# Two cached decode attentions on one core: the keys of the second loaded whole in 64 KB rows, with part of them copied aside by GpSimd, and its softmax taken in two halves

## The chip, the core and the metric

The kernel runs on one core of one Trainium2 chip. A core has a matrix engine (TensorE, PE in the profile), a vector engine (VectorE, DVE), a scalar engine (ScalarE, ACT), GpSimd (POOL) and SyncE (SP), which issues transfers. They share the on-chip memories SBUF (128 partitions) and PSUM (where PE writes), and 16 DMA engines bring data from HBM into SBUF. Engines run their own instruction lists and wait for each other by semaphores. The metric is the device time of one execution in microseconds (us).

## The reference

Two independent attention steps for one new token, A and B, each for a batch of 4, 32 query heads and a head size of 128, in bf16. Their results are laid side by side in the output of shape (4, 1, 1024).

```
q = (x @ wq) split into 32 heads
scores = q . k / sqrt(128);  p = softmax(scores);  o = p . v;  result = concat(o) @ wo
A: 8 key/value heads (each shared by 4 query heads), the last 2048 of 8192 cached positions
B: 32 key/value heads, all 8192 cached positions
```

B's caches are 256 MB of keys and 256 MB of values (4 x 32 x 8192 x 128 in bf16 each), so nearly all of the kernel is the reading and use of B's caches.

## The kernel before, in words

The work is cut into 40 chunks. Chunks 0 to 7 are A's. Chunks 8 to 39 are B's (the code's `NCA` is 8 and `NC` is 40): each is four heads of one batch entry, so 256 key tiles and 256 value tiles of 128 x 128. Four chunks in a row (the four batch entries) share one slice of B's output weights, `wos`, of 0.5 MB.

SBUF holds one long buffer `kv` of ten slots, 16 KB in each partition. In part B the keys of a chunk fill slots 0 to 3 (64 KB in each partition), the values slots 4 to 7; slot 8 holds `wol`, the reordered output weights. There is one buffer for keys and one for values. The keys come as two transfers of half a chunk, so in rows of 32 KB, the values as one transfer in rows of 64 KB. Only the last chunks are loaded in more pieces (`LASTK`, `NEXTK`, `LASTV`, `NEXTV`), so that their use can begin earlier.

SP issues all these transfers in the order of the chunks, keys before values, and each waits until the part of the buffer that it overwrites has been used: a half of the keys until the transposes of that half of the chunk before are done, the values until the last product with the values of the chunk before is done. POOL does nothing in part B but pass landings on: it waits for a transfer's semaphore and raises a counter (`r_k`, `r_v`; `relay`, L70) that PE waits for.

`whole_B` (L796) writes one chunk for all engines:

- For each group of 8 key tiles (32 groups), PE transposes the tiles into one of three PSUM banks `tr` (`emit_T`, L465), DVE (two groups of three) or ACT (the third) copies the bank to `kt` in SBUF (L486, L484), and two groups later PE multiplies them with the query into the scores `sc` (`emit_S`, L503). DVE also copies the query of the chunk into `qq` (`emit_qb`, L491).
- After the last scores the softmax follows over the whole chunk. `stats_rowmax` (L546) takes the maxima per partition of both halves, `stats_gmax` (L561) turns them by PE and reduces them, `stats_bc` (L579) spreads the maximum of each head to its partitions, and `exp_B` (L595) takes the exponentials, 8 instructions on ACT. While that runs, PE reorders the output weights (`reorder`, L706, 16 matmuls in all; DVE copies the result to `wol`, `take_wol`, L714) and does 11 matmuls on constants that only keep it busy (`keep_busy`, L791).
- PE multiplies the probabilities with the 256 value tiles (`emit_pv`, L643), DVE sums the probabilities (`sums_B`, L605), PE sums over partitions (`norm_sum`, L662) and DVE scales the result (`norm_out`, L680).
- The product with the output weights (`emit_fin`, L719) is done by PE two groups into the next chunk, and for the last chunk behind the loop.

The order is written out by hand. `emit_looped` (L156) looks for equal stretches between the marks set by `mark` and makes a loop of each engine's equal chunks; on PE and DVE one loop covers all 32 chunks of B. What differs between chunks only by steps of semaphore values is put into registers.

The lines that the steps of the prediction touch are L363 to L411 (transfers of B and their order), L465 to L489, L546 to L607, L643 to L717 and L796 to L832.

Of the kernel before, what the change touches and what calls it, by code (L numbers as in the profile page):

```python
# [5 lines left out]

ACTF = mybir.ActivationFunctionType
# [5 lines left out]
P = 128  # L13
# [9 lines left out]
LASTK = (32, 32, 64, 64, 64)  # L23
NEXTK = (64, 64, 64, 64)
NEXTV = (128, 64, 32, 32)
LASTV = (128, 64, 32, 16, 8, 8)
QK = (0, 4, 8, 16, 24)
QV = (0, 16, 24, 28, 30, 31)

# [139 lines left out]
def bass_concat_heads__sliding_block_cached__mha_block_cached__decode_kernel(  # L169
# [42 lines left out]
    assert sum(LASTV) == sum(LASTK) == sum(NEXTK) == sum(NEXTV) == NTB and NTA * 16 == 1024 and NTB * 4 == 1024  # L212

    sch = _Sched()
    with ExitStack() as es:
# [26 lines left out]
        rh = sb("rh", [P, 2, 4], F32)  # L242
# [4 lines left out]
        rst = {0: sb("rsa", [P, NSM, 16], F32), 1: sb("rsb", [P, 4], F32)}  # L247
# [3 lines left out]
        pbt = {0: sb("pba", [P, NPB, NTA * 16 + NW], BF16), 1: sb("pbb", [P, 1, NTB * 4 + NW], BF16)}  # L251
# [6 lines left out]
        wol = kv[:, 8, 0:4 * DO].rearrange("p (u n) -> p u n", u=4)  # L258
        tr = ps("tr", [P, NTRB, TG * P], BF16)
# [4 lines left out]
        xtps = ms[:, XT0:XT0 + KC * NB].bitcast(BF16)  # L264

        semnames = ["eng_pe", "eng_dve", "eng_act", "eng_pool", "eng_sp", "d_x0", "d_x1", "d_o0", "d_o1", "r_k", "r_v"]
        semnames += ["d_h%d" % i for i in range(NH)] + ["d_bk0", "d_bk1", "d_bv0"]
        semnames += [f + str(i) for f, x in (("d_lk", LASTK), ("d_nk", NEXTK), ("d_lv", LASTV), ("d_nv", NEXTV)) for i in range(len(x))]
# [79 lines left out]
        def dma_wos(hq):  # L348


            src = B_wo[4 * hq * P:4 * (hq + 1) * P, :].rearrange("(p r) n -> p (r n)", r=4)
            sch.add_dma("sp", lambda e: e.dma_start(wos[:, :, :].rearrange("p r n -> p (r n)"), src), "d_wos",
                        waits=[("reord", NCA + 4 * hq - 1)] if hq else [], key=("wos", hq))
# [9 lines left out]
        def dma_B(kind, c, part=None):  # L363


            ch = chunks[c]
            T, at, steps = (B_k, KB, QK) if kind == "k" else (B_v, VB, QV)
            src = T[ch["b"], 4 * ch["hq"]:4 * ch["hq"] + 4].rearrange("u (pp j) d -> (u pp) (j d)", pp=P // 4)
            dst = flat(at, 4)
            if kind == "k":  # L370
                pieces, fam = (LASTK, "d_lk") if c == NC - 1 else (NEXTK, "d_nk") if c == NC - 2 else ((NTB // 2,) * 2, "d_bk")
            else:
                pieces, fam = (LASTV, "d_lv") if c == NC - 1 else (NEXTV, "d_nv") if c in (NC - 2, NC - 3) else ((NTB,), "d_bv")
            j0, unit, used = 0, NTB // 4, {}
            for i, n in enumerate(pieces):
                if part is not None and i != part:
                    j0 += n
                    continue
                waits = []
                for u in range(j0 // unit, (j0 + n - 1) // unit + 1):  # L380
                    waits += held[at + u]
                    used[at + u] = [("T", ch["s"] + (u + 1) * unit // TG - 1) if kind == "k" else ("pv", c)]
                x = slice(j0 * P, (j0 + n) * P)
                sch.add_dma("sp", lambda e, x=x: e.dma_start(dst[:, x], src[:, x]), fam + str(i), waits=waits, key=(kind, c, i))
                j0 += n
                sch.relay("pool", sems, "r_" + kind, n // TG, [(kind, c, i)] + ([("wos", ch["hq"])] if i == 1 and kind == "k" and ch["b"] == 0 else []))
            for g, end in zip(steps, steps[1:] + (NTB // TG,)):
                sch.tk[(kind + "r", c, g)] = ("r_" + kind, (c - NCA) * (NTB // TG) + end)
            for u in used:
                held[u] = used[u]  # L390
# [527 lines left out]
```

## Time and profile before

| | |
|---|---|
| device time, 3 runs | median 1375.0 us (1374.14 to 1376.61) |
| profiled execution, first to last instruction (its span) | 1371.8 us |
| PE busy, share of the span | 1249.8 us, 91% |
| DVE busy | 744.0 us, 54% |
| ACT busy | 513.8 us, 37% |
| POOL busy | 9.8 us, 1% |
| read from HBM | 587.21 MB, 428 GB/s over the span |

The profile gives one execution and its span; the 3.2 us between the span and the median of the runs lie around it. In the rows that follow, times are in us from the start of the span. A row of the timeline gives the start, the length, the engine, the line, the operation, what is written from what, how many instructions were merged, and in brackets how long the engine had been idle before and what released it. "issue" as a releaser means that nothing that the profile shows was waited for. PE is the matrix product, PEld its loading of weights. A row of a window gives, for each engine, its busy time and instructions, then the granted clock of PE (1.00 is full), the mean busy share of the DMA engines and their rate.

### The profile page before, as it was taken

Reading aid. Unit: us, or ns where it says so; the run is one execution under the profiler, and the core shown is the slowest. Engines: PE = TensorE matmul, PEld = TensorE weight load, DVE = VectorE, ACT = ScalarE, POOL = GpSimd, SP = SyncE. Lnnn points to the kernel's source line nnn. Section 1 sums busy time; section 2 is a strip of 40 time slices with the busy share of each in tenths; the row PEclk is TensorE's granted clock in tenths of the full one; section 3 lists DMA queues with packets and bytes.
Section 4 is the critical chain, followed back from the end, with each engine's and each line's share of the span. In section 5 each row is a group of like instructions: output and inputs, shape, how many; then the busy total and the mean of one; then the engine's idle time right before and its main releaser. Section 6 shows DMA issues by size and latency. Waiting matters only on the chain.

```text
span 1371.8 us, 61526 instructions
## 1 busy us (share of the span) xinstructions
PE 1249.8 (91%) x27769; PEld 1110.4 (81%) x27769; DVE 744.0 (54%) x1335; ACT 513.8 (37%) x649; POOL 9.8 (1%) x29
## 2 busy tenths in 40 slices
PE   4897999998999999999999999999999999998998
PEld 4786788888778787888777888888778889877887
DVE  1675456655545556555555555554555555554555
ACT  1553244433333344333333443333333433333333
POOL 2000000000000000000000000000000000000000
PEclk9998899999999999999999999999999999999999
DMA  9999999999999999999999999999999999999998
GB/s 398 427 426 444 417 422 431 432 437 441 428 438 428 423 434 434 431 438 440 428 428 424 438 431 429 445 432 428 434 429 429 430 438 438 434 430 429 422 428 340
DMA packets 21084, 587.52 MB, mean 428 GB/s; under 512 B 2356, under 2 KB 2376, under 8 KB 4808
## 3 DMA queue, kind: packets, MB, share of 16 engines
q1 hardware_dynamic: 21032, 587.21, 99.6%
q8 instruction: 15, 0.25, 0.1%
q14 instruction: 5, 0.04, 0.0%
q10 hardware_dynamic: 32, 0.01, 0.0%
HBM read 587.21 MB, written 0.01 MB: 428 GB/s over the span
## 4 chain that ended last, share of the span: by engine, by line
DMA 57%; PE 39%; DVE 2%; issue 1%; ACT 0%; SPq 0%; POOLq 0%; DVEq 0%
DMA kv<-in_B_k_cache_dram 36%; DMA kv<-in_B_v_cache_dram 18%; PE tr L419 18%; PE po L421 9%; PE sc L421 8%; DMA kv<-in_B_wq_dram 2%; PE fin L421 1%; PE ms L421 1%; PE tr L421 1%; DMA kv<-in_A_k_cache_dram 1%; DVE sA L539 1%; DVE kt L486 0%; DVE kv L716 0%; ACT pba L623 0%; DVE rm L551 0%
## 5 line engine op out<-in xcount | busy, mean ns | idle before, releaser
L419 PE MATMUL tr<-identb,kv 128*128 128x128 bf16 x8704 | 668.6, 221 | 48.2 <-POOLq L72 42.3
L486 DVE COPY kt<-tr 128x1024 bf16<-128x1024 bf16 x736 | 501.9, 691 | 264.0 <-PE tr L419 261.3
L484 ACT ACTIVATE kt<-tr 128x1024 bf16<-128x1024 bf16 x352 | 359.3, 1023 | 703.5 <-PE tr L419 703.4
L419 PEld LDWEIGHTS tr<-identb,kv 128*128 128x128 bf16 x8704 | 510.3, 99 | 61.1 <-DVE qq L495 41.2
L421 PE MATMUL sc<-qq,kt 128*128 128x64 bf16 x8192 | 399.3, 192 | 13.5 <-DVE kt L486 9.8
L421 PEld LDWEIGHTS sc<-qq,kt 128*128 128x128 bf16 x8192 | 332.9, 98 | 16.9 <-DVE kt L486 13.1
L421 PEld LDWEIGHTS po<-pbb,kv 128*128 128x128 bf16 x8192 | 250.9, 99 | 37.1 <-issue 20.5
L421 PE MATMUL po<-pbb,kv 128*128 128x64 bf16 x8192 | 253.8, 194 | 24.1 <-POOLq L72 22.6
L601 ACT ACTIVATE pbb<-sc,negb 32x128 bf16<-32x128 f32 x256 | 137.8, 538 | 136.3 <-DVE negb L584 133.0
L421 PE MATMUL po<-sel,identb 128*128 128x512 bf16 x352 | 96.9, 384 | 0.0
L716 DVE CAST kv<-tr 128x512 bf16<-128x512 f32 x128 | 80.0, 683 | 0.0
L606 DVE TENSOR_REDUCE rsb<-pbb 128x4 f32<-128x1024 bf16 x32 | 39.0, 1220 | 65.8 <-ACT pbb L601 65.8
L421 PE MATMUL tr<-wos,back 32*128 32x512 bf16 x512 | 67.8, 383 | 3.2
L421 PEld LDWEIGHTS po<-sel,identb 128*128 128x128 bf16 x352 | 26.6, 98 | 47.6 <-issue 27.8
L668 DVE RECIPROCAL rinv<-ms 128x4 f32<-128x4 f32 (+1 forms) x40 | 7.8, 196 | 105.6 <-PE ms L421 105.6
L555 DVE TENSOR_REDUCE rh<-sc 128x4 f32<-128x512 f32 x64 | 43.9, 686 | 14.3 <-PE sc L421 14.3
L421 PEld LDWEIGHTS tr<-wos,back 32*128 32x128 bf16 x512 | 21.5, 93 | 34.0 <-DVE kv L716 18.9
L690 DVE TENSOR_TENSOR oz<-po,rz 128x16 bf16<-128x16 f32 x32 | 5.6, 175 | 67.9 <-PE po L421 67.9
L570 DVE TENSOR_REDUCE gm<-ms 4x4 f32<-4x128 f32 x40 | 11.2, 279 | 28.6 <-PE ms L419 28.6
L421 PE MATMUL sc<-qb,kt 128*128 128x64 bf16 (+3 forms) x512 | 26.3, 197 | 0.4 <-DVE gx L576 0.4
L421 PEld LDWEIGHTS ms<-gm,ind 4*128 4x128 f32 x64 | 9.4, 182 | 17.5 <-DVE gm L570 17.5
L421 PEld LDWEIGHTS sc<-qb,kt 128*128 128x128 bf16 x512 | 22.1, 102 | 1.6 <-issue 0.9
(65 smaller groups left out, 250.4 us busy)
## 6 DMA issues: line engine op xcount, KB each, us to landing
kv<-in_B_k_cache_dram SPq DMA_DIRECT2D x60, 4096.0 KB, 27.4
kv<-in_A_k_cache_dram SPq DMA_DIRECT2D x8, 2048.0 KB, 13.0
kv<-in_A_v_cache_dram SPq DMA_DIRECT2D x8, 2048.0 KB, 14.6
kv<-in_B_k_cache_dram SPq DMA_DIRECT2D x7, 2048.0 KB, 28.4
kv<-in_B_v_cache_dram SPq DMA_DIRECT2D x3, 4096.0 KB, 22.3
kv<-in_B_v_cache_dram SPq DMA_DIRECT2D x3, 2048.0 KB, 26.8
kv<-in_B_v_cache_dram SPq DMA_DIRECT2D x5, 1024.0 KB, 29.6
kv<-in_A_wq_dram SPq DMA_DIRECT2D x1, 4096.0 KB, 12.5
```

Of the source, the lines that this page charges most:

```text
L419: sch.add("pe", lambda e: e.transpose(o, l, r), waits, key)
L421: sch.add("pe", lambda e: e.matmul(o, l, r, start=start, stop=stop), waits, key)
L484: sch.add("act", lambda e: e.activation(dst, src, ACTF.Copy), waits=waits, key=("ev", s))
L486: sch.add("dve", lambda e: e.tensor_copy(dst, src), waits=waits, key=("ev", s))
L539: emit = lambda e, src=src, b=b: e.scalar_tensor_tensor(out=t, in0=src, scalar=mk[:, b:b + 1], in1=t, op0=ALU.mult, op1=ALU.add)
L555: sch.add("dve", lambda e: e.tensor_reduce(out=rh[:, half, :], in_=src, axis=AX.X, op=ALU.max), waits=[("S", ch["s"] + (half + 1) * ch["NG ...
L570: sch.add("dve", lambda e: e.tensor_reduce(out=gm[0:C, m, 0:U], in_=src, axis=AX.X, op=ALU.max), waits=[("trm", c)], key=("gmax", c))
L601: sch.add("act", lambda e, src=src, dst=dst, pp=pp, u=u: e.activation(dst, src, ACTF.Exp, bias=negb[pp, 0, u:u + 1], scale=scale), waits=[ ...
L606: sch.add("dve", lambda e: e.tensor_reduce(out=rst[1][:, :], in_=probs_of(c).rearrange("p j u -> p u j"), axis=AX.X, op=ALU.add), waits=[( ...
L668: sch.add("dve", lambda e: e.reciprocal(out=ri, in_=ms[:, L0:L0 + n]), waits=[("L", c)], key=("rinv", c))
L690: sch.add("dve", lambda e: e.tensor_tensor(out=o, in0=i0, in1=i1, op=ALU.mult), waits=waits, key=("oT", c))
L716: sch.add("dve", lambda e: e.tensor_copy(wol[:, u, :], o), waits=[("reord", c) if u == 3 else ("reord", c, u)] + [("fin", prev(c))], key=( ...
```

## The change

- B's keys are loaded as one transfer of 8 MB in rows of 64 KB for 26 of the 32 chunks (9 to 34). Chunk 8 comes in pieces of 128, 32 and 96 tiles, chunks 35 to 38 in pieces of 64, 96 and 96, chunk 39 in 32, 32, 96 and 96. Values come in pieces of 128, 64 and 64 tiles in chunks 35 to 38.
- A second place `kspare` for the last 96 key tiles of a chunk lies in slots 8 and 9. After a whole load has landed, POOL copies these 96 tiles there in 12 instructions of 8 tiles (`land_kB`), and PE transposes them from there. So the load of the next keys waits for the transposes of the first 160 tiles and for the 12 copies of the chunk before; in chunks with pieces, the last 96 tiles are loaded into `kspare` directly.
- The softmax of a chunk has two halves. The first half's maximum is taken while the transposes go on, and its exponentials (groups 23 and 26) too. The second half uses the larger of both maxima. The products with the values of the first half (in `po`) start right behind the last scores; those of the second half go to another bank (`po2`, in `tr`). A factor from the difference of the two maxima (`weigh_B`) brings the first half's sums and products to the scale of the second (`rest_sums`, `norm_sum`, `add_first`).
- The output product of a chunk (`emit_fin`) is now at the end of the same chunk, followed by all 16 matmuls of `reorder` for the next chunk and 3 `keep_busy` matmuls; `take_wol` stands at the head of the next chunk on DVE. The first three transposes of a chunk wait for `take_wol`.
- The query copy of a chunk moves from DVE to ACT. POOL's relays are listed in a loop of their own, with one more counter for `wos`. In the changed program PE's loop covers 31 of B's chunks; the last chunk is written out behind it, since the product that closes the sum in `emit_fin` (`stop`) now lies inside it.

The core of the diff:

```diff
-LASTK = (32, 32, 64, 64, 64)
-NEXTK = (64, 64, 64, 64)
-NEXTV = (128, 64, 32, 32)
+KMAIN = 160
+FIRSTK = (128, 32, 96)
+LATEK = (64, 96, 96)
+LASTK = (32, 32, 96, 96)
+NLATE = 5
+NEXTV = (128, 64, 64)
...
+        kspare = kv[:, 8:10, :].rearrange("p s x -> p (s x)")[:, 4 * DO:4 * DO + (NTB - KMAIN) * P]
...
+        po2 = tr[:, 2, :].bitcast(F32)
...
+        def kpieces(c):
+            return FIRSTK if c == NCA else LASTK if c == NC - 1 else LATEK if c >= NC - NLATE else (NTB,)
...
+                    dst = flat(KB, 4)[:, j0 * P:(j0 + n) * P]
+                    if c == NCA:
+                        waits = held[0] + held[1] + held[2] + held[3]
+                    else:
+                        waits = [("T", s0 + min(j0 + n, KMAIN) // TG - 1)]
+                        if j0 + n > KMAIN and len(kpieces(c - 1)) == 1:
+                            waits += [("cp", c - 1)]
...
+        def land_kB(c):
...
+                if len(pieces) == 1:
+                    sch.relay("pool", sems, "r_k", KMAIN // TG, [("k", c, i)])
+                    for g in range(NCP):
+                        x = slice((KMAIN + g * TG) * P, (KMAIN + (g + 1) * TG) * P)
+                        dst, org = kspare[:, g * TG * P:(g + 1) * TG * P].bitcast(I32), flat(KB, 4)[:, x].bitcast(I32)
+                        sch.add("pool", lambda e, dst=dst, org=org: e.tensor_copy(dst, org), waits=[("T", s0 + ch["NG"] - 1)] if g == 0 else [])
+                        emit, waits, _, at = sch.ops["pool"][-1]
+                        sch.ops["pool"][-1] = (emit, waits, ("r_c", 1), at)
...
+        def weigh_B(c):
+
+            sch.add("dve", lambda e: e.tensor_tensor(out=e01[:, :], in0=negb[:, 1, :], in1=negb[:, 0, :], op=ALU.subtract),
+                    waits=[("negb", c, 1)] + ([("rse", c - 1)] if c > NCA else []), key=("d01", c))
+            sch.add("act", lambda e: e.activation(e01[:, :], e01[:, :], ACTF.Exp), waits=[("d01", c)], key=("e01", c))
...
+        def add_first(c):
+
+            pe_mm(po2[:, 0:4], identf[:, :], t1[:, :], start=False, stop=False, waits=[("t1", c)], key=("add", c))
+            po_read[:] = [("t1", c)]
...
         def whole_B(c):
...
             sch.mark()
+            take_wol(c)
             emit_qb(c)
             for g in range(ch["NG"]):
                 emit_T(ch["s"] + g)
-                if g == 1:
-                    emit_fin(p)
                 if g >= SLAG:
                     emit_S(ch["s"] + g - SLAG)
-                if g == ch["NG"] // 2 + SLAG + 1:
+                if g == 18:
                     stats_rowmax(c, 0)
+                if g == 20:
+                    stats_gmax(c, 0)
+                if g == 22:
+                    stats_bc(c, 0)
+                if g == 23:
+                    exp_B(c, 0, (0, 1))
+                if g == 26:
+                    exp_B(c, 0, (2, 3))
             for g in range(SLAG):
                 emit_S(ch["s_last"] + 1 - SLAG + g)
             stats_rowmax(c, 1)
-            reorder(c, 0, 0)
-            reorder(c, 1, 1)
-            reorder(c, 2, 2)
-            keep_busy(2)
-            stats_gmax(c)
-            keep_busy(1)
-            stats_bc(c)
-            exp_B(c)
-            for u in range(3):
-                take_wol(c, u, u)
-            keep_busy(3)
-            reorder(c, 3, 0)
-            keep_busy(5)
-            take_wol(c, 3, 0)
-            sums_B(c)
             for g in range(ch["NG"]):
                 emit_pv(c, g)
-                if g == 20:
+                if g == 4:
+                    stats_gmax(c, 1)
+                if g == 8:
+                    stats_bc(c, 1)
+                    sums_B(c, 0)
+                    exp_B(c, 1, (0, 1, 2, 3))
+                    weigh_B(c)
+                    sums_B(c, 1)
+                    rest_sums(c)
+                if g == 24:
                     norm_sum(c)
+                if g == ch["NG"] - 2:
+                    add_first(c)
             norm_out(c)
+            emit_fin(c)
+            reorder(c + 1)
+            keep_busy(NBUSY)
...
         finish_A()
+        reorder(NCA)
         for c in range(NCA, NC):
             whole_B(c)
         sch.mark()
-        emit_fin(NC - 1)
+        emit_out(NC - 1)
```

284 lines of the change are left out of this document (176 added, 108 removed).

## The prediction

> **What bounds the kernel now.** I read the page first: the slices of the DMA engines and the share of the queue that loads the caches.
>
> ```profile
> span 1371.8 us, 61526 instructions
> ...
> DMA  9999999999999999999999999999999999999998
> ...
> q1 hardware_dynamic: 21032, 587.21, 99.6%
> ```
>
> Every slice but the last has the DMA engines busy at 90% or more, and the loading queue fills 99.6% of 16 engines over a span of 1371.8 us. Nothing that only makes an engine faster can shorten this. The time is the bytes, the price of their packets, gaps in the queue, and what follows the last byte. To see how late PE may be, I read PE's timeline over one chunk of B in mid run.
>
> ```profile
> 672.88 1.06 PE L419 MATMUL tr<-identb,kv 128*128 128x128 bf16 x16 [1.85 <-POOLq L72]
> ...
> 695.76 1.06 PE L421 MATMUL tr<-wos,back 32*128 32x512 bf16 x12
> ...
> 699.08 1.03 PE L421 MATMUL tr<-wos,back 32*128 32x512 bf16 x4
> ...
> 701.96 5.06 PE L421 MATMUL po<-pbb,kv 128*128 128x64 bf16 x168 [0.67 <-POOLq L72]
> ...
> 711.66 0.51 PE L419 MATMUL tr<-identb,kv 128*128 128x128 bf16 x6 [1.85 <-POOLq L72]
> ```
>
> The chunk lasts from 672.88 to 711.66, 38.78 us. PE waits only for landings that POOL passes on: 1.85 us for keys, 0.67 us for values. Without them its own chain is 38.78 - 1.85 - 0.67 = 36.26 us, 2.5 us below the transfers' period.
>
> **Packets.** A window of the DMA view in mid run, then the same row of a window in part A, whose rows are shorter.
>
> ```profile
> DMA packets 10666, 389.04 MB, mean 432 GB/s; under 512 B 1184, under 2 KB 1184, under 8 KB 1824
> ...
> q1 hardware_dynamic: 10664, 389.03, 100.2%
> ```
>
> ```profile
> q1 hardware_dynamic: 2294, 25.53, 100.4%
> ```
>
> The first has 27.4 packets and (900 us x 16 x 1.002 / 389.03 MB =) 37.09 us of engine time per MB, the second 89.9 packets and (60 x 16 x 1.004 / 25.53 =) 37.75. The difference, 0.66 us over 62.5 packets, is 10.6 ns a packet. A transfer of B has 128 rows and 16 small packets (1184 in that window for its 74 transfers). The 26 whole key loads each save one transfer's 144 packets, 3744 in all; the pieces of chunks 8, 35 to 39 (keys) and 35 to 38 (values) come to 576 more by the change's lists. So 3168 fewer, x 10.6 ns / 16 = **-2.1 us**. Bounds: 0, if two short rows cost no more than a long one here, and -2.9, if only half of the added small pieces count and a packet costs 13 ns.
>
> **Does the queue stay full?** A whole key load may start when the first 160 tiles of the chunk before are transposed and POOL's 12 copies are done. The rows of the operations concerned, by shape:
>
> ```profile
> L486 DVE COPY kt<-tr 128x1024 bf16<-128x1024 bf16 x736 | 501.9, 691 | 264.0 <-PE tr L419 261.3
> ...
> L601 ACT ACTIVATE pbb<-sc,negb 32x128 bf16<-32x128 f32 x256 | 137.8, 538 | 136.3 <-DVE negb L584 133.0
> ...
> L716 DVE CAST kv<-tr 128x512 bf16<-128x512 f32 x128 | 80.0, 683 | 0.0
> ...
> L308 POOL TENSOR_SCALAR_AFFINE_SELECT back<-back 128x512 bf16<-128x512 bf16 x4 | 2.5, 634 | 0.6
> L295 POOL MEMSET pba<- 128x2176 bf16 x1 | 1.9, 1912 | 0.0
> ```
>
> Transposes and scores take from 672.88 to 695.76, 22.9 us for 32 groups, about 0.7 us each; 20 groups and the start come to some 14 us behind the keys' landing. The values behind these keys need 8.39 MB at 432 GB/s = 19.4 us. At the end of the first pass of B the values' buffer was freed at 169.59 (first pass, below), and the DMA share was low for the next stretch:
>
> ```profile
> 169.00:171.00 2.00, 2.00 (x47) 1.71 (x43) 0.75 (x3) 0.00 (x0) 0.00 (x0) 1.00 0.80 311
> ```
>
> So from freeing a buffer to full engines it is roughly 1.6 us (estimate), and the deadline is 19.4 - 1.6 = 17.8 us behind the landing. The transposes meet it by almost 4 us. The copies: no row shows a POOL copy from SBUF. Nearest are POOL's select of 128x512 elements, 634 ns, the same number of elements as one copy here (8 tiles as 512 integers a partition), and as the far end the memset of 2176 elements, 1912 ns. I take 0.63 us: 12 x 0.63 = 7.6 us, done long before the transposes. The point from which copies decide is 17.8 / 12, about 1.45 us. The landing of the values is queued behind the copies on POOL; it comes 19.4 us after the keys, so it waits for nothing up to 1.6 us a copy. I cost the copies at **0**; the cover is the transposes.
>
> [...]
>
> The first load of part B's values after that low stretch can go earlier now, as the first half's products start earlier: 0.4 us of idle engines in that row, of which I take **-0.3** (bounds -0.6 and +1, since PE's first pass is paced by its code, below, and may be later still).
>
> **PE's chain.** Moved and added parts, each against 38.78 us. Transposes and scores: 22.9. Stats of the first half lie inside them; DVE there has 23 x 0.691 + 4 x 0.683 = 18.6 us of 22.9, so the casts of the weights that move to the head of the chunk, and the first half's maximum, fit. Products: 256 tiles at 5.06 / 168 us each are 7.7, with the second half's softmax beside the first half's products. Its length shows in ACT's row of the same chunk:
>
> ```profile
> 698.46 4.41 ACT L601 ACTIVATE pbb<-sc,negb 32x128 bf16<-32x128 f32 x8 [4.06 <-DVE negb L584]
> ```
>
> Scores ended at 695.76 at the latest, the exponentials began at 698.46, and four of them are 4 x 0.538 = 2.2 us: 4.9 in all, against 3.9 us for 128 tiles. I take a stall of 1.0 and 0.7 for the sums and the addition: 9.4. Output product and scaling 1.0 (estimate). The 16 reorder matmuls now stand together, 1.0 us (12 took 1.06, 4 took 1.03). The casts, 2.7 us, stand ahead of the next chunk's first copies on DVE, and PE's first transposes wait for them: 2.1 at most if PE came without a pause. Sum 36.4 us, 2.4 below the period, so **0**. The cover is PE's wait for keys, some 4 us between chunks, in which the casts are done too; without it PE would set the period. The sum may be 1.5 higher (estimate) where PE's clock drops: behind a wait of the same length as at 672.88, another chunk started with
>
> ```profile
> 398.88 1.65 PE L419 MATMUL tr<-identb,kv 128*128 128x128 bf16 x16 [1.86 <-POOLq L72]
> ```
>
> 1.65 us where 1.06 stood. Still below 38.78. Products end at 22.9 + 0.7 + 9.4 = 33.0 behind the keys' landing, 13.6 behind the values', where they ended 8 behind (709.81 against 701.96). The load of the next values has 17.8, so it isn't late. In the last five chunks, with pieces, PE must make up these 5 us: it gains about 2.4 a chunk, so it is level at the last. The query copy on ACT stands behind the second half's exponentials and has the rest of the products to be done in: 0.
>
> **The tail.** Before:
>
> ```profile
> 1366.00:1367.00 1.00, 1.00 (x41) 1.00 (x38) 0.24 (x2) 0.00 (x0) 0.00 (x0) 1.00 0.08 31
> ```
>
> ```profile
> 1365.70 2.73 PE L421 MATMUL po<-pbb,kv 128*128 128x64 bf16 x88
> ...
> 1368.47 0.17 DVE L690 TENSOR_TENSOR oz<-po,rz 128x16 bf16<-128x16 f32 x1 [2.07 <-PE po L421]
> ```
>
> The data end near 1366.8, the products at 1368.43, 1.6 us behind, and the output path takes 3.3 us more to 1371.8. With the first half's products ahead of the second softmax, PE should be level with the data but for the last tiles: **-0.9** (bounds 0 and -1.4).
>
> **Code.** PE's loop covered all 32 chunks, and its code came in during the first pass: window of that pass, and PE's timeline in it.
>
> ```profile
> q8 instruction: 7, 0.11, 0.9%
> ```
>
> ```profile
> 122.34 1.06 PE L419 MATMUL tr<-identb,kv 128*128 128x128 bf16 x16
> ...
> 137.20 0.34 PE L421 MATMUL sc<-qq,kt 128*128 128x64 bf16 x3 [3.68 <-issue]
> ...
> 169.59 1.06 PE L419 MATMUL tr<-identb,kv 128*128 128x128 bf16 x16
> ```
>
> The pass took 169.59 - 122.34 = 47.25 us, 11.0 over the free chain, with 7 code packets of 16 KB and waits such as 3.68 us for no releaser but "issue". The window 300 to 1200 has 10666 - 10664 = 2 packets outside the loading queue, far from 7 a chunk: the loop stays loaded. The changed loop covers 31 chunks and the last one is written out behind it, so it is fetched again, beside saturated DMA engines, where nothing follows to hide it. [...] PE's waits for the last pieces of keys absorb one chunk's slack, 2.5 to 2.9. I take **+5.5** (bounds 0, if fetching runs ahead of PE, and +10).
>
> [...]
>
> **Sum.** -2.1 - 0.3 + 0 - 0.9 + 5.5 = +2.2 us: span 1374.0. The runs' median lies 3.2 us above the span of before (1375.0 - 1371.8), so 1377.2 us.
>
> **The rivals.** B, the code is hidden: the rows of the last loads are short pieces, so a code packet waits less than behind 32 and 64 KB rows, and fetching may run ahead in PE's 4 us of idle time. For it: seven code packets made few waits as long as the 3.68 us. Against it: the pass as a whole was 11 us long. Time: 1374.0 - 5.5 = 1368.5, +3.2 = 1371.7, faster. [...] E, that the queue doesn't go faster with longer rows, is the bound 0 of the first term: 1379.3, inside the forecast's range.
>
> **How the numbers follow.** About 0.2%, 2.75 us, is what a measurement of this kernel can tell from no change; so same is 1372.25 to 1377.75. Forecast (1374.5 to 1380): 53%, of it same 26, slower 25, faster 2 for a better packet price. B (1370.5 to 1373): 24%, of it faster 17, same 7. C: 8%, slower. D: 15%, slower, but 1 for a small one that ends as same. That is faster 0.19, same 0.34, slower 0.47. The range leaves out C and the far ends of B and D: 1370.5 to 1386. Cases of both signs hold chances, so the likeliest one's own range is 1374.5 to 1380.
>
> **What would show it.** Packets: 3168 fewer on the loading queue, and a chunk period near 38.70. [...] PE: one wait of about 4 us between chunks, a stall of about 1 us in the products. Code: some 5 more packets on the queue of instructions after 1320, and PE waits for "issue" in the last chunk that sum to 5 or more; if there are none, B. The prediction is wrong in kind if the DMA share has gaps in mid run, or if PE's wait between chunks is gone.

## The result, and the profile after

| | before | after |
|---|---|---|
| median of 5 runs | 1374.1 us | 1383.3 us (1379.0 to 1384.4) |
| ratio to before, 95% interval | | 1.0064 (1.0052 to 1.0077) |
| span of the profiled execution | 1371.8 us | 1381.5 us |
| last byte of the caches landed | 1366.8 us | 1374.1 us |

The change makes the kernel 0.64% slower. The time lies inside the range, 6 us above the forecast of 1377.2. "Before" was run again beside every group of experiments and its median lay between 1372.6 and 1374.1, so kernels of different groups are compared by their ratios to it. The changed kernel's profiled execution took 1383.3 us, 1.8 more than its span, and this distance is 1.7 to 1.8 us in the executions of before too. So of the 3.2 us between span and median before, which the prediction added, 1.4 were only the difference between the profiled execution and the median.

The page of the changed kernel, beside the rows of before that open the prediction:

```profile
span 1381.5 us, 62503 instructions
...
DMA  9999999999999999999999999999999999999997
...
q1 hardware_dynamic: 17864, 587.21, 98.9%
q8 instruction: 22, 0.36, 0.1%
```

The loading queue lost its 3168 packets (17864 against 21032). Still its share fell from 99.6% to 98.9% of a longer span, and the last slice is emptier. There are 22 code packets (0.36 MB of instructions, 16 KB each) where there were 15. The next four parts say where time was won and lost.

**Mid run, the packets.** PE's rows of two chunk starts, both released by landed keys; the columns are start, length, instruction, count and the wait with its releaser:

```profile
453.32 1.60 PE L487 MATMUL tr<-identb,kv 128*128 128x128 bf16 x24 [3.44 <-POOLq L78]
...
492.03 2.66 PE L487 MATMUL tr<-identb,kv 128*128 128x128 bf16 x24 [2.17 <-POOLq L78]
```

They lie 38.71 us apart where before had 38.78. A whole key load lands 19.35 us after the load ahead of it, two halves took 9.71 each. The difference, 0.075 us before rounding, is 2.0 us won over 26 chunks.

**The first pass of B.** The window 160 to 180 of before, then of after. The last three columns are PE's granted clock, the mean share of the DMA engines and their GB/s:

```profile
160.00:180.00 20.00, 18.59 (x493) 17.87 (x492) 8.64 (x15) 6.02 (x9) 0.00 (x0) 1.00 1.02 429
```

```profile
160.00:180.00 20.00, 14.72 (x284) 12.47 (x283) 6.08 (x18) 3.14 (x7) 6.51 (x12) 0.80 0.77 317
```

The share of 0.77 is 4.6 us in which the engines were idle. The last byte of chunk 9's values came 24.3 us behind that of its keys, against 20.5 before, where a load of 8 MB takes 19.35 in mid run: 3.8 us more than before. PE's rows of the pass and the code packets of 122 to 182:

```profile
122.87 0.37 PE L489 MATMUL po<-wos,back 32*128 32x512 bf16 x1
128.57 2.74 PE L487 MATMUL tr<-identb,kv 128*128 128x128 bf16 x24 [5.33 <-issue]
...
166.34 1.83 PE L489 MATMUL po<-pbb,kv 128*128 128x64 bf16 x31 [3.37 <-issue]
```

```profile
q8 instruction: 8, 0.13, 0.9%
```

PE stood still for 5.33 us at the first transposes of B, for no releaser but "issue". Before had no wait there and 7 packets in that window. Its first pass began at 122.34, this one 6.2 us later, and it took no longer from there on. The pass's last products ended at 174.8, and only then may the next values be loaded; before issued them at 169.7.

**Late key loads.** PE's rows of two chunk starts, SP's issues of the key loads that follow, the window behind the second issue, and windows of the first 14 us of these two chunks and of a third:

```profile
569.44 1.66 PE L487 MATMUL tr<-identb,kv 128*128 128x128 bf16 x24 [3.63 <-POOLq L78]
...
609.43 2.74 PE L487 MATMUL tr<-identb,kv 128*128 128x128 bf16 x24 [3.48 <-POOLq L78]
```

```profile
584.08 0.33 SPq L403 DMA_DIRECT2D kv<-in_B_k_cache_dram  x1
...
625.10 0.33 SPq L403 DMA_DIRECT2D kv<-in_B_k_cache_dram  x1
```

```profile
628.00:630.00 2.00, 2.00 (x51) 2.00 (x49) 0.98 (x3) 1.64 (x3) 0.00 (x0) 1.00 0.80 328
```

```profile
569.44:583.44 14.00, 14.00 (x288) 13.93 (x289) 8.19 (x13) 5.80 (x6) 6.73 (x12) 0.88 1.02 440
609.43:623.43 14.00, 14.00 (x262) 14.00 (x263) 7.87 (x12) 5.12 (x5) 6.73 (x12) 0.80 1.02 440
687.93:701.93 14.00, 14.00 (x321) 13.86 (x322) 9.63 (x15) 6.27 (x7) 6.74 (x12) 1.00 1.04 449
```

The granted clock over the first 14 us is 0.88 in the first chunk, 0.80 in the second and 1.00 in the third. Their successors' keys are issued 14.6, 15.7 and 13.2 us behind the start. Behind the second issue the DMA share drops to 0.80, and this load came 20.2 us behind the one ahead of it, 0.9 late. The other two came on time. Six loads between 230 and 830 are late like this (keys, and the values behind them), 4.0 us in all. Four chunk starts between 200 and 1150 have a clock of 0.80 to 0.82 over their first 14 us (217, 609, 767 and 1040). Behind the first three the keys came late; behind the fourth they were on time, as a load of weights still stood in the queue. All other chunks of that stretch issued within 14.7 us and no key load behind them was late.

**The end.** PE's last chunk:

```profile
1347.90 0.62 PE L487 MATMUL tr<-identb,kv 128*128 128x128 bf16 x8 [2.67 <-POOLq L78]
...
1370.31 0.71 PE L489 MATMUL po<-pbb,kv 128*128 128x64 bf16 x19 [0.79 <-issue]
...
1378.53 0.60 PE L489 MATMUL fin<-kv,oz 128*4 128x256 bf16 x8 [0.36 <-DVE oz L797]
```

The 2.67 us stand under a landing, the 0.79 us under "issue"; a code packet came in during the first (1345.6) and ahead of the second (1367.9). Behind the first wait the clock fell:

```profile
1348.00:1355.00 7.00, 7.00 (x129) 7.00 (x129) 2.84 (x5) 2.81 (x3) 0.00 (x0) 0.76 1.03 441
```

The last output product starts 4.4 us behind the last byte (1374.1), where before it started 2.0 behind it (1368.79 against 1366.8). From the last byte to the end of the span it is 7.4 us against 5.0.

The sum: 3.8 for the first pass, 4.0 for late keys, -2.0 for packets and 2.4 at the end are 8.2 of the 9.7 us by which the span grew. The other 1.5 lies in the loads of the last chunk. The third piece of its keys (96 tiles) landed 9.0 us behind the second, where such a piece takes 7.3 in the chunks before, and the first of the six late code packets came in this stretch. The experiments show that these packets are the cause.

### The profile page after: what moved, and what is told of

It reads as the page before. It is cut to its first block, busy times and chain, and to the rows that moved or that the text cites. A ratio compares the mean times of both kernels' runs of the same rounds, so it can differ in the third digit from the quotient of the medians.

```text
span 1381.5 us, 62503 instructions
## 1 busy us (share of the span) xinstructions
PE 1204.2 (87%) x27648; PEld 1128.3 (82%) x27681; DVE 770.3 (56%) x1559; ACT 520.7 (38%) x713; POOL 185.3 (13%) x341
## 3 DMA queue, kind: packets, MB, share of 16 engines
q1 hardware_dynamic: 17864, 587.21, 98.9%
## 4 chain that ended last, share of the span: by engine, by line
DMA 51%; PE 44%; issue 3%; DVE 2%; ACT 0%; SPq 0%; ACTq 0%; POOLq 0%; DVEq 0%
DMA kv<-in_B_k_cache_dram 49%; PE tr L487 26%; PE sc L489 12%; PE tr L489 2%; DMA kv<-in_B_wq_dram 2%; PE po L489 2%; PE ms L489 1%; PE fin L489 1%; DVE kt L558 1%; DVE sA L611 1%; DVE kv L830 0%; ACT pbb L680 0%; DVE rm L623 0%; PE ms L487 0%; DVE sA L609 0%
## 5 line engine op out<-in xcount | busy, mean ns | idle before, releaser
L487 PEld LDWEIGHTS tr<-identb,kv 128*128 128x128 bf16 x8704 | 531.7, 101 | 108.9 <-issue 66.7
L489 PE MATMUL sc<-qq,kt 128*128 128x64 bf16 x8192 | 404.7, 193 | 14.7 <-DVE kt L558 13.2
L418 POOL COPY kv<-kv 128x512 int32<-128x512 int32 x312 | 175.4, 620 | 977.2 <-DMA kv<-in_B_k_cache_dram 977.2
L489 PE MATMUL tr<-pbb,kv 128*128 128x64 bf16 x4096 | 137.0, 194 | 27.1 <-ACT pbb L680 25.5
L489 PEld LDWEIGHTS tr<-pbb,kv 128*128 128x128 bf16 x4096 | 132.3, 100 | 31.0 <-issue 28.2
L489 PE MATMUL po<-pbb,kv 128*128 128x64 bf16 x4096 | 136.0, 194 | 4.2 <-issue 4.2
L489 PEld LDWEIGHTS po<-pbb,kv 128*128 128x128 bf16 x4096 | 128.4, 99 | 5.4 <-issue 4.4
L687 DVE TENSOR_REDUCE rs<-pbb 128x4 f32<-128x512 bf16 x32 | 21.9, 686 | 50.3 <-ACT pbb L680 50.3
L489 PE MATMUL tr<-wos,back 32*128 32x512 bf16 x396 | 34.9, 377 | 0.0
L489 PE MATMUL po<-wos,back 32*128 32x512 bf16 x132 | 34.1, 377 | 0.0
L628 DVE TENSOR_REDUCE rh<-sc 128x4 f32<-128x512 f32 x32 | 22.1, 691 | 14.3 <-PE sc L489 14.3
```

What stands on the lines that cost most here:

```text
L418: sch.add("pool", lambda e, dst=dst, org=org: e.tensor_copy(dst, org), waits=[("T", s0 + ch["NG"] - 1)] if g == 0 else [])
L487: sch.add("pe", lambda e: e.transpose(o, l, r), waits, key)
L489: sch.add("pe", lambda e: e.matmul(o, l, r, start=start, stop=stop), waits, key)
L628: sch.add("dve", lambda e: e.tensor_reduce(out=dst, in_=src, axis=AX.X, op=ALU.max), waits=[("S", ch["s"] + (half + 1) * ch["NG"] // 2 - 1 ...
L687: sch.add("dve", lambda e: e.tensor_reduce(out=dst, in_=probs_of(c, half).rearrange("p j u -> p u j"), axis=AX.X, op=ALU.add), waits=[("ex ...
```

## The experiments

Theory **G** was that gaps in the loading queue are most of the loss, theory **L** (the forecast) that the code of the last chunk is. The first four kernels tell them apart. Ratios are to before, with their 95% intervals; the change itself has 1.0064 (1.0052 to 1.0077).

### e1_loop32: PE's loop over all chunks

```diff
-                          stop=i == len(ops) - 1 and c == lastc, ...
+                          stop=ab == 0 and i == len(ops) - 1 and c == lastc, ...
...
+                    pe_mm(fin[...], pbt[1][:, 0, NTB * 2:NTB * 2 + NB], rhs[...], start=False, stop=True, ...)
```

> The changed kernel with one thing undone: no product of emit_fin closes its sum inside the chunk (two products with a zero operand close it behind the last chunk), so PE's loop covers all 32 chunks and the last one is not written out. Theory L (the forecast: the code of the last chunk costs 5.5 us and is most of the loss): no code packet near the end, no wait for 'issue' in the last chunk, median 1383.3 - 5.5 = 1377.8, and the time behind the last data falls from 7.4 to about 2 to 3 us. Theory G (the loss is mostly gaps in the loading queue, at the end of the first pass and where a key load is issued late): the last data stay near 1374.1, products cannot end before them, so only 3 to 4 us are won: about 1379.5 to 1380.5. Rival (PE is late at the end for want of slack, and code has no part): within 1 us of 1383.

Measured: 1.0072 (1.0059 to 1.0085), no gain. The six late code packets are gone and so is every wait for "issue" in the last chunk, but the edit put a cost of its own in their place. PE's rows of the end:

```profile
1376.31 0.60 PE L489 MATMUL fin<-kv,oz 128*4 128x256 bf16 x8 [0.27 <-DVE oz L797]
...
1378.60 0.27 PE L489 MATMUL fin<-sel,pbb 128*4 128x256 bf16 x2
```

The closing products stand behind reorder and keep_busy, 1.7 us behind the output product, and the output waits for them; in the changed kernel it doesn't wait for reorder. The output product itself starts 1.2 us behind the last byte (1375.1) instead of 4.4, 3.2 us won. The loads of the last chunk are faster too: from the landing of the second piece of its keys to the last landing they take 34.2 us, where the change takes 35.7. (The same 34.2 is found in e5_loop32b, e8_combo, e9_tiny and e11_best, which have no late code packets either; the other kernels with these pieces and with such packets take 34.8 to 35.8.) So the code of the last chunk costs 1.5 us in the queue and 3.2 at the end, 4.7 together, and theory L explains about half of the loss. In all nothing was won, as the end behind the output product became 2.0 us longer, the late key loads of this profile make 5.9 us instead of 4.0, and the gap of the first pass is 0.6 larger.

### e2_v9: the values of chunk 9 in pieces

```diff
-... (NEXTV, "d_nv") if c >= NC - NLATE else ((NTB,), "d_bv")
+... (NEXTV, "d_nv") if c >= NC - NLATE or c == NCA + 1 else ((NTB,), "d_bv")
```

> The changed kernel with the values of chunk 9 loaded in pieces of 128, 64 and 64 tiles as in the late chunks; everything else as it is. The first piece then waits for the products of the first half of chunk 8 only (ended near 168.0 in the changed kernel's trace) and not for the last ones (174.8). Theory G: the idle DMA time between 160 and 180, 4.85 us in the changed kernel against 0.62 before, falls below 1 us, the last data come about 4 us earlier and the median is about 1379.3. Rival (the gap is given back later, since PE then sets the pace or a later key load is late in its place): last data within 1 us of 1374.1, median 1382 to 1384.

Measured: 1.0058 (1.0045 to 1.0071). The window 160 to 180:

```profile
160.00:180.00 20.00, 14.67 (x324) 12.39 (x322) 6.57 (x20) 2.47 (x7) 6.43 (x12) 0.91 0.95 397
```

The gap is closed (0.95 against 0.77), but the last byte came only 1.4 us earlier, at 1372.7. The pass is still long, so the keys of chunk 10 were issued late instead (1.3 us, and 0.4 for the values behind them), and other late loads cost 4.9 us where the first profile had 4.0. Closing the gap at the transfer moves it on. What makes PE late has to go.

### e3_busy11: PE kept busy through its wait

```diff
-NBUSY = 3
+NBUSY = 11
```

> The changed kernel with 11 keep_busy products behind each chunk instead of 3, about 2.4 us more of PE's wait for keys filled. Theory G with the clock: chunks start at full clock, so 160 tiles are transposed 13 to 14 us behind the keys' landing and not 15.7, the late key loads (single extra gaps of 0.3 to 1.4 us, 4.0 in all by the landings) disappear, and with PE faster in the last chunk the median falls by 3 to 4, to about 1379.5. Rival 1 (the clock does not follow from PE's wait): as many starts with 2.6 to 2.7 us for 24 transposes as before, median unchanged. Rival 2 (the products come too late for short waits and delay the transposes): chunks start later, median 1384 or more.

Measured: 1.0065 (1.0053 to 1.0078), no change, by two effects against each other. The granted clock over the span:

```profile
core 0: 1381.4 us, clock 0.975
```

It was 0.959 in the changed kernel. Late key loads fell from 4.0 to 1.1 us by the landings, as the clock theory says: no chunk behind the first pass has a clock below 0.87 over its first 14 us. In exchange the first pass, which has no slack, got 1.6 us longer, and the end of the span lies 8.9 us behind the last byte instead of 7.4: the products are on PE's path in the last chunks, where a chunk without a wait for keys takes 36.6 us instead of 36.0. The 3 to 4 us that were expected did not come, as the second rival's cost ate what the clock won.

### e4_k192: the deadline of a key load

```diff
-KMAIN = 160
+KMAIN = 192
```

> The changed kernel with 192 key tiles in the first place and 64 in the second (8 copies instead of 12), so a whole key load waits for 24 groups of transposes instead of 20, about 2.7 us more; the pieces are cut at 192 too. By the forecast's deadline of 17.8 us behind the landing (1.6 us from issue to full engines) the load would be issued at 16.7 to 18.4: time within 1 to 10 us of 1383. Theory G (the deadline is about 15.3, some 4 us from issue to full engines, as the extra gaps at issues 15.7 us behind a landing say): every whole load leaves 1.4 to 3 us of idle queue, 26 x that, 1420 to 1460. If copies had been what is late, 8 instead of 12 would make it faster.

Measured: 1.0399 (1.0386 to 1.0413), 1427.8 us. A start of a chunk on PE, and SP's issue of the keys that follow:

```profile
580.21 2.74 PE L487 MATMUL tr<-identb,kv 128*128 128x128 bf16 x24 [4.40 <-POOLq L78]
```

```profile
598.53 0.33 SPq L403 DMA_DIRECT2D kv<-in_B_k_cache_dram  x1
```

The issue is 18.3 us behind the start, where the latest behind the first pass of the changed kernel is 15.7, and behind the first pass the landings are late by 42 us in all, 1.6 for each whole load. So the forecast's deadline of 17.8 us was too late: at 14.7 there is no gap in the changed kernel, at 15.7 one of 0.9. Fewer copies made nothing faster.

### e5_loop32b: reorder at the head of the chunk, loop over all chunks

```diff
             sch.mark()
+            reorder(c)
+            keep_busy(NBUSY)
             take_wol(c)
...
             emit_fin(c)
-            reorder(c + 1)
-            keep_busy(NBUSY)
```

(and the closing products of e1_loop32 behind the loop; `reorder(NCA)` ahead of the loop is gone)

> As e1_loop32, but with reorder and keep_busy at the head of a chunk instead of its end, so that the two closing products follow the last output product at once (in e1_loop32 they stood 1.7 us behind it, in the path to the output). PE's loop covers all 32 chunks. Theory: the last chunk's code costs about 3 us in the changed kernel (its products end 5.0 behind the last data, those of e1_loop32 1.8), less 0.5 for the closing products: tail behind the last data about 4.9 instead of 7.4, median 1380.5 to 1381 with the gaps of the queue as in the changed kernel. Forecast: 5.5 less, 1377.8. Rival (no part of the loss is code): 1383.

Measured: 1.0015 (1.0006 to 1.0024), 1374.9 us. This wins back three quarters of the loss, more than expected. The first window, and PE at the end:

```profile
160.00:180.00 20.00, 15.55 (x335) 13.57 (x335) 7.31 (x16) 2.05 (x2) 6.50 (x12) 0.91 0.96 402
```

```profile
1340.57 0.62 PE L487 MATMUL tr<-identb,kv 128*128 128x128 bf16 x8 [0.82 <-POOLq L78]
...
1368.17 0.60 PE L489 MATMUL fin<-kv,oz 128*4 128x256 bf16 x8 [0.27 <-DVE oz L797]
```

```profile
q8 instruction: 15, 0.25, 0.1%
```

The end is as expected: in the last chunk PE waits 0.82 us for keys, never for "issue", no code packet comes after the 15 of the first passes, and the output product starts 1.2 us behind the last byte (1366.95). The surprise is the first window: 0.96 against 0.77, the next values issued at 170.6 instead of 174.8. The 5.33 us at the first transposes are gone, although reorder and the transposes run in the same order. What differs there is that reorder's 16 products (and 3 of keep_busy) lie inside the loop and not in front of it. e9_tiny tests that.

### e6_before_last: the code alone, in the kernel before

```diff
-            keep_busy(2)
+            keep_busy(2, c == NC - 1)
```

(the flag only picks another constant of the same shape, so that the last chunk no longer equals the others)

> The kernel before with the last chunk written out behind PE's loop, as the change has it: two keep_busy products of the last chunk use another constant of the same shape, nothing else differs. This prices the code by itself. Forecast's term: +5.5 (0 to 10). Theory after the first runs: 5 or 6 code packets at the end, waits for 'issue' of 2 to 4 us in all, +2 to +5 by how much of them falls on PE's waits for data. Rival: PE waits for data anyway, +0.

Measured: 1.0014 (1.0005 to 1.0023), +1.9 us. PE at the end and the code packets of 1300 to 1372:

```profile
1367.74 0.73 PE L421 MATMUL po<-pbb,kv 128*128 128x64 bf16 x19 [1.14 <-issue]
...
1371.53 0.60 PE L421 MATMUL fin<-kv,oz 128*4 128x256 bf16 x8 [0.27 <-DVE oz L690]
```

```profile
q8 instruction: 6, 0.10, 0.6%
```

Six packets, as in the change, and waits for "issue" of 1.14 and 0.49 us. The output product starts 3.0 us behind the last byte, before it was 2.0. The last byte itself came 1.7 us later (1368.5). By the landings 0.5 of that had gathered before the last chunk, in passes that the edit doesn't touch. The other 1.2 came within the last chunk, 0.9 of it at the piece of keys during which the first of the six packets arrived (1338.4): it landed 5.8 us behind the piece ahead, where 64 tiles take 4.9. So the code alone costs 1.2 us in the queue and 1.0 at the end here, 2.2 together; in the changed kernel it was 1.5 and 3.2.

### e7_kpieces: keys in pieces throughout

```diff
-... LATEK if c >= NC - NLATE else (NTB,)
+... LATEK if c > NCA else (NTB,)
```

> The changed kernel with the keys of chunks 9 to 34 in pieces of 64, 96 and 96 as in the late chunks, so no whole load and no copies by GpSimd, and the first piece may be issued after 8 groups of transposes instead of 20. Values, softmax and code as in the changed kernel. Theory G: the late key loads disappear (4.0 us by the landings, among them 1.5 at chunks 10 and 11), the gap at the end of the first pass stays at 4 to 6; packets rise by 2 x 144 x 26 x 10.6 ns / 16 = 5.0 us: median 1384 (1382.5 to 1386). If late key loads are no cost of their own, 1388; if a packet costs nothing, 1379.

Measured: 1.0047 (1.0034 to 1.006). The loading queue on its page:

```profile
q1 hardware_dynamic: 25352, 587.22, 99.2%
```

By the landings no key load is late, and the gap of the first pass is as large as in the change (5.0). A chunk's keys land in 19.50 us in three pieces and in 19.35 in one. Over 26 chunks this is 3.8 us for 7488 more packets, 8.2 ns each and not 10.6, so 3.8 of the 5.0 us expected. Still the last byte came 0.5 us earlier (1373.6), as the 4.0 us of late loads were won.

### e8_combo and e11_best: towards a faster kernel

e8_combo is e5_loop32b with values of chunk 9 and keys of chunk 10 in pieces and longer keep_busy; e11_best has fewer chunks in pieces. Against e5_loop32b:

```diff
 e8_combo
-NBUSY = 3
+NBUSY = 7
-... LATEK if c >= NC - NLATE else (NTB,)
+... LATEK if c >= NC - NLATE or c == NCA + 2 else (NTB,)
-... NEXTV if c >= NC - NLATE else (NTB,)
+... NEXTV if c >= NC - NLATE or c == NCA + 1 else (NTB,)
 e11_best
-NLATE = 5
+NLATE = 4
-NBUSY = 3
+NBUSY = 7
```

> All that the runs so far suggest, in the changed kernel: values of chunk 9 in pieces (e2), keys of chunk 10 in pieces, PE's loop over all 32 chunks (e5), 7 keep_busy products. Theory G: gap 160 to 180 under 1 us, late key loads under 2 us in all, last data near 1367.5, tail near 5: span 1372 to 1374, median 1374 to 1376, so level with the kernel before or up to 0.2% slower, as the packets win 2 and the closing products, the larger pieces and the remaining gaps give it back. Rival (PE's chain is what bounds the changed kernel, gaps only show it): above 1379.

> e5_loop32b with 7 keep_busy products instead of 3 and 4 late chunks instead of 5 in pieces. Theory: late key loads (3.2 us by the landings in e5_loop32b, 2.4 of them in mid run) fall under 1, 4 x 144 packets less win 0.4, PE is still level at the end: 1372.5 to 1373.5, 0 to 0.1% faster than before. Rival (the 1.2 us of products are on PE's path in the last chunks and 4 chunks don't suffice to make up for it): 1374 to 1376.

Measured: e8_combo 0.9997 (0.9987 to 1.0007), e11_best 1.0010 (1.0000 to 1.0021). Both are level with before or nearly. e8_combo's last byte lands at 1366.1, 0.7 us earlier than before's, and its end is 4.3 us behind it. In e11_best, which has the same keep_busy, the end is 5.5 behind, as its rival said: with four chunks in pieces instead of five PE isn't level in time. The late key loads are 1.1 and 1.2 us in these two kernels, as in e3_busy11 with 11 products; in the seven kernels with whole loads and 3 products (e4_k192 left out) they are 2.0 to 6.9. No kernel here is faster than before by more than the measurement can tell.

### e9_tiny: the place of the loop's code

```diff
         finish_A()
+        for _ in range(16):
+            pe_mm(sc[:, 1, 0:4], identb[:, :], identb[:, 0:4])
         for c in range(NCA, NC):
```

> e5_loop32b with 16 products of 4 columns more between part A and PE's loop, so the loop begins 16 products later in PE's code, as in the changed kernel, where reorder(8) stands there; the loop itself is that of e5_loop32b. Theory P (place of the code: those instructions push the loop's first code packet out of reach, as the wait of 5.33 us for 'issue' at the first transposes and 8 code packets instead of 7 in the changed kernel say): a wait of about 5 us at the first transposes of chunk 8, idle DMA of 4 to 5 us between 160 and 180 instead of 1.05, median 1379 to 1381. Rival (e5_loop32b won in the first pass because reorder is out of the way of the softmax or the transposes, not by place): no such wait, median 1375 to 1376.

Measured: 1.0049 (1.0036 to 1.0062), +0.34% over e5_loop32b. PE around the sixteen products, the code packets of 122 to 182, and the first window:

```profile
123.08 0.58 PE L489 MATMUL sc<-identb 128*128 128x4 bf16 x16
129.98 0.63 PE L489 MATMUL tr<-wos,back 32*128 32x512 bf16 x3 [6.31 <-issue]
```

```profile
q8 instruction: 8, 0.13, 0.9%
```

```profile
160.00:180.00 20.00, 14.69 (x351) 14.06 (x348) 6.65 (x18) 4.44 (x9) 6.43 (x12) 0.83 0.53 229
```

The products take 0.58 us. Behind them PE waits 6.31 us for "issue", at the first instruction of the loop, and there are 8 packets instead of 7. So what cost the first pass was where the loop's code begins, not what stands in it. The gap between 160 and 180 is larger than expected (a share of 0.53, where the change has 0.77). But the profiled execution was the slowest of the five (1385.3), so the ratio is the better measure.

### e10_head: reorder moved, the last chunk written out

e5_loop32b without the closing products, so `stop` stays in `emit_fin`; against the changed kernel:

```diff
+            reorder(c)
+            keep_busy(NBUSY)
             take_wol(c)
...
-            reorder(c + 1)
-            keep_busy(NBUSY)
```

(and `reorder(NCA)` ahead of the loop is gone)

> The changed kernel with reorder and keep_busy at the head of a chunk, as in e5_loop32b, but with the closing product inside the last chunk, which is therefore written out behind the loop as in the change. So the first pass is that of e5_loop32b and the last chunk that of the changed kernel. Theory: two costs of code that add up. Idle DMA between 160 and 180 about 1, last data near 1367 to 1368, six code packets and waits for 'issue' in the last chunk, tail behind the last data 7, median 1377 to 1378.5: 2.5 to 3 us over e5_loop32b and 5 to 6 below the change. Rival (the last chunk's code only matters when PE is late from the first pass on): 1375 to 1376.

Measured: 1.0044 (1.0032 to 1.0056), 1379.9 us. The first window:

```profile
160.00:180.00 20.00, 15.40 (x328) 13.26 (x329) 7.83 (x18) 2.86 (x5) 6.59 (x12) 0.91 0.94 392
```

The first pass is that of e5_loop32b (0.94), the six packets at the end are back, the loads of the last chunk take 35.4 us instead of 34.2, and the end is 6.2 us behind the last byte (4.3 in e5_loop32b). The median is 2 us above what was expected: in its profile late key loads make 5.4 us by the landings, against 2.2 in e5_loop32b, though both have the same rule for them. Over e5_loop32b, the loop's place (e9_tiny) costs 0.34% and the last chunk's code (this kernel) 0.29%; the changed kernel, which has both, lies 0.49% over it. So the two costs add up as far as the intervals, some 0.13% on each ratio, can tell.

### e12_twice: copies for nearly twice as long

```diff
+                        if g < 8:
+                            sch.add("pool", lambda e, dst=dst, org=org: e.tensor_copy(dst, org), waits=[("one", c, g)])
```

> The changed kernel with the first 8 of the 12 copies of a chunk made twice by GpSimd, so that copying lasts 11 to 13 us instead of 6.75 behind the keys' landing, still less than the 13.9 to 15.7 us to the transposes that the next load waits for as well. Theory: covered, no change beyond the spread of the changed kernel, 1380 to 1385, VectorE's copies stay at 690 ns. Rival (copies are on the path, or GpSimd and VectorE get in each other's way): every load is later by up to 6 us, 1400 and more, or VectorE's copies longer than 700 ns.

Measured: 1.0057 (1.0041 to 1.0073), no loss against the change. The groups of copies by shape:

```profile
L560 DVE COPY kt<-tr 128x1024 bf16<-128x1024 bf16 x736 | 502.9, 690 | 291.6 <-PE tr L489 289.0
...
L418 POOL COPY kv<-kv 128x512 int32<-128x512 int32 x312 | 187.9, 617 | 841.4 <-DMA kv<-in_B_k_cache_dram 841.4
L420 POOL COPY kv<-kv 128x512 int32<-128x512 int32 x208 | 128.2, 617 | 12.8
```

Copying lasts 12.2 us behind the landing (6.75 in the change), and no load waits for it, as the transposes take 13.2 us or more. VectorE's copies stay at 690 ns beside it.

## Why the prediction was right, and where it was wrong

By its own steps:

- **Packets, -2.1.** Right in kind, a little too large: the 26 whole loads won 2.0 where 10.6 ns a packet gives 2.5. By the period of a chunk a packet costs 8.3 ns, by e7_kpieces 8.2. The 576 packets that the late pieces add, 0.3 us at this price, are too little to be told apart. (The bound of -2.9 comes to -2.8 by its own terms.)
- **The queue stays full, copies cost 0.** The copies were right:

```profile
L558 DVE COPY kt<-tr 128x1024 bf16<-128x1024 bf16 x736 | 503.2, 690 | 298.6 <-PE tr L487 295.8
...
L418 POOL COPY kv<-kv 128x512 int32<-128x512 int32 x312 | 175.4, 620 | 977.2 <-DMA kv<-in_B_k_cache_dram 977.2
```

  620 ns a copy (0.63 was taken), done 6.75 us behind the landing, and e12_twice shows the cover. (The point from which copies decide, 17.8 / 12, is 1.48 us and not 1.45.) Beside GpSimd's copies VectorE's copies out of PSUM took 690 ns, as before (691). So the low share of the DMA engines at a key load's start (0.80 from 628 to 630) isn't the copies' doing here.

  The step failed in its deadline. "So from freeing a buffer to full engines it is roughly 1.6 us (estimate)" came from one window in which the mean share was read as one idle stretch. The kernel before held a better measure: the values issued at 169.70 had 3.3 us to the last byte ahead of them (173.0) and still came 1.1 us late (20.5 us instead of 19.35). With that the deadline is near 15 us (19.4 - 3.3 - 1.1) and not 17.8, which e4_k192 and the late loads bear out: 14.7 is in time, 15.7 is not. At full clock the transposes had some 2 us to spare, not "almost 4", and half clock over the start of a chunk (0.50 from 609.43 to 613.00), which the step left out, cost 2.5 us (15.7 against 13.2). Size: 0 forecast, 4.0 in the profile.
- **First pass, -0.3.** This step failed too: it cost 3.8. The prediction counted 11 us of code loading in the first pass of before and gave the changed pass the same or less. It named "PE's first pass is paced by its code" as a bound of +1. What it missed is that moving reorder(8) in front of the loop shifts the loop's code. e5_loop32b and e9_tiny show it from both sides. The counts show one more code packet between 122 and 182 where sixteen products stand in front of the loop (8 in the changed kernel and in e9_tiny, 7 in before and in e5_loop32b). Why sixteen decide was not shown.
- **PE's chain, 0 in mid run.** Right: PE waits 2 to 4 us for keys between chunks, a chunk without such a wait takes 36.0 us where 36.4 was summed, and the stall for the second softmax is 0.83 us where 1.0 was taken.
- **The tail, -0.9.** Right where the code doesn't disturb it: in e5_loop32b the output product starts 1.2 us behind the last byte, before 2.0.
- **Code of the last chunk, +5.5.** Right in kind (six packets) and nearly in size: 1.5 us in the last chunk's loads and 3.2 at the end (4.4 - 1.2, by comparing with e5_loop32b), 4.7 together. No run shows the 5.5 itself, the part of a first pass's 11.0 us that the last chunk was to cost; in its place the runs showed six packets from 1345.6 on and these 4.7 us. The way there was another. PE's waits for "issue" in that chunk sum to 1.1 us (0.31 and 0.79), where 5 or more were to be the sign. The rest fits the late third piece of keys and the low clock behind the longer wait for it (0.76 over 7 us); no run prices these two apart. In the kernel before the same code costs 2.2.

So the sign held, and the code of the last chunk was about half of the 9.7 us. What failed are two terms that the prediction had put at nothing: the full queue (0, but 4.0, by the deadline) and the first pass (-0.3, but 3.8, by the place of the loop's code). By its own sign, gaps in the DMA share in mid run, the prediction was wrong in kind there. That the time still lies in the range is partly luck. The range's upper end, 1386, stood for a PE that isn't level at the end (D), and that isn't the reason here: with its code in the loop PE is level (e5_loop32b: the output product 1.2 us behind the last byte). A low clock did matter, though through the key loads.

What stays open: why PE starts some chunks at full and some at half clock behind waits of the same length (1.00 at 923.9 behind 3.46 us, 0.50 at 609.4 behind 3.48), and so why late key loads vary between 2.0 and 6.9 us in kernels with the same rule for them. That more keep_busy brings them down to 1.1 is shown by e3_busy11, which changes nothing else; e8_combo and e11_best agree.

## What to carry to other kernels

When a change moves instructions in front of a loop or out of one, price the loop's first pass and the code behind it as steps of their own: here sixteen products in the wrong place cost 5 us, and a last chunk that no longer equals the others 2 to 5. When a reload's issue is moved later, take its deadline from an issue that was late in the trace, not from a mean share of the engines, and ask what a slow start does to it. A saving of 2 us shows only after those are at zero.

## What the runs showed of the hardware

A whole load had to be issued some 4 us before the queue ran dry (estimate from these loads): one issued 3.1 us ahead of the last byte in the queue (625.1 against 628.2) came 0.9 late, one 4.1 us ahead (468.0 against 472.1) came on time. One added code packet at a loop's start went with a wait of PE of 5.3 to 6.3 us, in the changed kernel beside full DMA engines (a share of 1.05 from 122.87 to 128.57), though a code packet itself took 1.1 us (8 of them 0.9% of 16 engines over 60 us). Late code packets made the loads of the last chunk 0.6 to 1.6 us longer (34.8 to 35.8 us instead of 34.2). Behind waits of 2 to 5.7 us PE started some chunks at full and some at low clock (24 transposes in 1.51 us at a clock of 1.00 from 687.93, in 2.74 at 0.50 from 609.43). GpSimd copied 512 integers a partition in 620 ns with no effect on VectorE's copies out of PSUM (690 ns).
